# Loads of v issued from POOL, and a later landing counted by a kernel's own scheduler

## The chip, the cores and the metric

The kernel runs on one core of one Trainium2 chip. Its engines are PE (matrix products), DVE (vector), ACT (activations), POOL and SP; each works through its own instructions strictly in order, and instructions on different engines wait for one another by semaphores. SP computes nothing here: its queue issues DMA transfers. The metric is the device time of one execution in microseconds; lower is better.

## The reference

What is computed is chunked local attention over 4 batches of 8 heads with 768 positions, and behind it two feed-forward layers (the names say "moe", but there is one expert):

```python
for c in range(nc):                      # chunks of 32 queries, 16 positions left, 8 right, 8 memory slots
    q_c = q[:, :, c_start:c_end]
    k_full = np.concatenate([mem_k, k[:, :, l_start:r_end]], axis=2)
    v_full = np.concatenate([mem_v, v[:, :, l_start:r_end]], axis=2)
    scores = scale * np.matmul(q_c, k_full.transpose(0, 1, 3, 2))
    a = np.exp(scores - np.max(scores, axis=-1, keepdims=True))
    a = a / (np.sum(a, axis=-1, keepdims=True) + 1e-09)
    out[:, :, c_start:c_end] = np.matmul(a, v_full)
x = out.transpose(0, 2, 1, 3).reshape(3072, 512)
x = (mish(x @ w_in1)) @ w_out1           # 512 -> 2048 -> 512; mish(h) = h * tanh(log(1 + exp(h)))
x = (h * sigmoid(1.702 * h)) @ w_out2    # h = x @ w_in2; 512 -> 2048 -> 512
```

## The kernel before

**Stages.** The 3072 tokens are cut into 8 blocks of 384. In the first phase, attention of the later blocks and the first product of layer 1 run side by side: `forward(j, f)` multiplies block j with column group f of w_in (16 groups), so this phase has 128 units, numbered i = 16 j + f; a unit is two halves of 6 matmuls (from block 1 on), accumulated in a bank `h`, copied to a tile `z` or `gl` (L1262, L1263, on ACT or DVE) and stored to DRAM as `g1d`. Behind it come the second product of layer 1 (L1393), the first of layer 2 (L1292) and the second of layer 2 (L1485), each by a seven-product scheme that needs sums and differences of weights. Products take a float32 operand as two parts, high and low, hence three matmuls for one product.

**Attention, from block 2 on.** `pair_of_heads` loads q and k in pieces (`z_...` and `wo_...` tiles; L364) and turns them on DVE (L658, L662); the few memory keys are copied in by POOL or DVE (L668). PE makes scores (L779), DVE adds the mask and finds the maximum (L837), ACT takes exponentials (L852), DVE or ACT scales them (L872, L880), PE turns the result (L983), and PE multiplies it with v (L1005). `values_of` loads v for half of the heads of a block: a tile `vt`, of which there are two, filled by 8 transfers (four of 120 rows of v, four of 8 memory rows; 10 at the sequence's end), 98 in all.

**Weights.** Beside it, the weights of the other three products are prepared on DVE, two tiles `v` and `u` at a time: shifts and ors (L408 to L422, L422 being the last), a store of both to DRAM (`wd`, SP), and then four sums or differences (L467) that overwrite what was stored, so that the first L467 must wait until the store has been read out of the tile; then a second pair of stores. Nine such groups fall between 97 and 350 us of the trace; two more groups are split on the chip and not stored.

**What sets the order.** Nothing is ordered by hand. The code adds operations to a `Plan` with a rank (in the first phase the number of the unit by which they are wanted), an engine or two to choose from, and a duration. `Plan.issue` walks through a clock of its own, gives each free engine the ready operation of lowest rank, and writes the instructions out in the order of the planned starts. A transfer in it occupies its issuing queue (0.475 us on SP), then a common bus, and whoever waits for it is ready a fixed time behind the bus: 1.1 us. Buffers are given back the same way. On the chip only the orders per engine are left of this plan; the times are the chip's. `CALM = 110` separates the first phase (ranks below it) from the rest.

Of the kernel before, what the change touches and what calls it, by code (L numbers as in the profile page):

```python
# [22 lines left out]
AHEAD = 6  # L23
CUT = 6
URGENT = 4
STAGGER = 1.5
LATE = 3

# [95 lines left out]
class Plan:  # L124
# [12 lines left out]
    def add(self, rank, ways, reads=(), writes=(), updates=(), chain=None, table=None):  # L137
        op = Op()
        op.table = table
        op.rank, op.seq = rank, len(self.ops)  # L140
        lap = self.OVERLAP if rank < self.CALM else {}
        op.ways = [(w[0], max(w[1] - lap.get(w[0], 0.0), 0.06), *w[2:]) for w in ways]
        op.after, op.at = [], 0.0
        need = {}

        def wait(o, lag=True):
            need[id(o)] = (o, lag or need.get(id(o), (o, False))[1])

        for b in (*reads, *updates):
            for o in b.writers:  # L150
                wait(o)
        for b in (*writes, *updates):
            for o in b.readers:
                wait(o)
            b = b.whole
            if not b.users and b.tag is not None:
                if b.inside is not None and b.inside.tag.made[0] is not b.inside:
                    below = b.inside.tag.made
                    k = below.index(b.inside)
                    b.gate += [(o, True) for o in below[k - 1].users]  # L160
                    below[k - 1].closed = True
                made = b.tag.made
                k = made.index(b)
                if isinstance(b.tag, Spread) and k < b.tag.bufs:
                    b.gate += [(o, True) for o in b.tag.before.get(b.inside, ())]
                if k >= b.tag.bufs:
                    b.gate += [(o, True) for o in made[k - b.tag.bufs].users]
                    made[k - b.tag.bufs].closed = True
                if k:
                    b.gate.append((made[k - 1].users[0], False))  # L170
        for b in writes:
            for o, lag in b.whole.gate:
                wait(o, lag)
        for b in updates:
            b.writers, b.readers = [], []
        for b in (*writes, *updates):
            b.writers.append(op)
        for b in reads:
            b.readers.append(op)
        for b in (*reads, *writes, *updates):  # L180
            assert not b.whole.closed
            b.whole.users.append(op)
            if b.whole.inside is not None:
                assert not b.whole.inside.closed
                b.whole.inside.users.append(op)
        if chain is not None:
            if chain:
                wait(chain[-1], False)
            chain.append(op)
        op.need = len(need)  # L190
        for o, lag in need.values():
            o.after.append((op, lag))
        self.ops.append(op)
        return op

    def issue(self):
        engines = ("pe", "act", "dve", "pool", "sp")
        free = dict.fromkeys(engines, 0.0)
        ready = {e: [] for e in engines}
        load = dict.fromkeys(engines, 0.0)  # L200
        coming = []
        bus = 0.0
        for op in self.ops:
            if op.need == 0:
                heapq.heappush(coming, (0.0, op.seq, op))
            op.start = None
        left = len(self.ops)
        now = 0.0
        table = None
        order = []  # L210
        while left:
            while coming and coming[0][0] <= now + 1e-9:
                op = heapq.heappop(coming)[2]
                for w, (e, dur, *_) in enumerate(op.ways):
                    heapq.heappush(ready[e], (op.rank, op.seq, w, op))
                load[op.ways[0][0]] += op.ways[0][1]
            for e in engines:
                if free[e] > now + 1e-9:
                    continue
                kept = []  # L220
                pick = other = None
                while ready[e]:
                    item = heapq.heappop(ready[e])
                    op, w = item[3], item[2]
                    if op.start is not None:
                        continue
                    if w:

                        e0, d0 = op.ways[0][:2]
                        if max(free[e0] - now, 0.0) + load[e0] - d0 < op.ways[w][1] - d0 + 0.3:  # L230
                            kept.append(item)
                            continue
                    if e == "act" and op.table not in (None, table):

                        if other is None:
                            other = item
                        else:
                            kept.append(item)
                        continue
                    pick = item  # L240
                    break
                if other is not None and (pick is None or other[0] + self.PATIENCE < pick[0]):
                    pick, other = other, pick
                if other is not None:
                    kept.append(other)
                for item in kept:
                    heapq.heappush(ready[e], item)
                if pick is None:
                    continue
                op, w = pick[3], pick[2]  # L250
                e_, dur, fn, *size = op.ways[w]
                op.start, op.way = now, w
                load[op.ways[0][0]] -= op.ways[0][1]
                order.append(op)
                left -= 1
                end = now + dur
                if e == "act" and op.table not in (None, table):
                    if table is not None:
                        end += self.RELOAD
                    table = op.table  # L260
                free[e] = end
                lag = self.LAG.get(e, 0.0)
                if op.rank < self.CALM:
                    lag += self.OVERLAP.get(e, 0.0)
                if size:
                    bus = max(bus, end + 0.9) + size[0]
                    end, lag = bus, 1.1
                for o, far in op.after:
                    t = end + lag if far else (now + 0.01 if not size else now + 0.01)
                    o.at = max(o.at, t)  # L270
                    o.need -= 1
                    if o.need == 0:
                        heapq.heappush(coming, (o.at, o.seq, o))
            times = [coming[0][0]] if coming else []
            times += [free[e] for e in engines if free[e] > now + 1e-9]
            if not times:
                assert not left, "operations wait for one another"
                break
            now = min(t for t in times if t > now) if any(t > now for t in times) else now
        order.sort(key=lambda o: (o.start, o.seq))  # L280
        for op in order:
            op.ways[op.way][2]()
# [15 lines left out]
def kernel(  # L298
# [14 lines left out]
    B, H, S, D = q.shape  # L313
# [4 lines left out]
    P = 128  # L318
# [6 lines left out]
    GB = TB // GQ  # L325
# [6 lines left out]
    HV = H // 2  # L332
# [10 lines left out]
    add = plan.add  # L343
# [12 lines left out]
    for f in range(NF):  # L356
        T.update(tags(sb, **{f"{n}{f}": 1 for n in ("wi", "wo")}))

    def load(rank, buf, parts, nbytes, run, reads=(), early=False):

        for part in parts:
            def go(queue, part=part):
                o, i = part()
                queue.dma_start(out=o, in_=i)  # L364

            size = bus(nbytes / len(parts), run)
            ways = [
                ("sp", 0.475, lambda go=go: go(nc.sync), size),
                ("pool", 1.2, lambda go=go: go(nc.gpsimd), size),
            ]  # L370
            add(rank, ways if early else ways[:1], reads=reads, writes=[buf])

# [311 lines left out]
    def values_of(j, hq, rank):  # L686

        b, s0 = divmod(j * TB, S)
        vt = T["vt"].new([P, GB, HV, D], F32)
        parts = []  # L690
        for i in range(GB):
            parts += windows(v, mem_v, b, s0 + i * GQ - LEFT, hq * HV, HV, vt, i)
        load(rank, vt, parts, P * GB * HV * D * 4, 256)
        return vt

    def windows(src, mem, b, t0, h0, nh, tile, i):
# [274 lines left out]
    def oct_out(j, rank, vt, heads):  # L971

        kept = []
        for hp, names, es, late in heads:
            aTs = []
            for n, e in enumerate(es):
# [7 lines left out]

                r = rank + late + STAGGER * n
                add(r + 2.2, [("pe", 0.33, turn)], reads=[e, ident], writes=[t])
# [648 lines left out]
```

## Time and profile before

| | us |
|---|---|
| median of 3 runs | 1133.25 (1132.56 to 1134.08) |
| the profiled execution, its own time | 1132.64 |
| its span, first to last instruction | 1130.3 |
| PE busy | 1101.3 (97%) |
| DVE busy | 855.3 (76%) |
| ACT busy | 593.9 (53%) |
| POOL busy | 14.6 (1%) |

PE is busy nearly throughout; what a change of order can move is the rest of its span. The mean granted TensorE clock is 0.994. The queue that SP fills carries 215.76 MB in 297759 packets, the one that POOL fills 0.75 MB in 352 packets, all of that in the first 15 us, where seven loads of block 0 go through POOL.

### The profile page before, as it was taken

The page shows a single profiled execution, that of the slowest core. Times are in us where ns is not written, and L with a number is a line of the kernel's source. Part 1 is how long each engine was busy: PE and PEld are TensorE (multiplying, and loading weights), DVE is VectorE, ACT ScalarE, POOL GpSimd, SP SyncE. Part 2 cuts the span into 40 slices and gives each one's busy share as a digit, 9 for nine tenths or more (in the row PEclk, how much of TensorE's full clock was granted, in tenths as well). Part 3 has the DMA queues.
Part 4 walks back from the last instruction along what each step waited for, and adds up shares of the span by engine and source line. Part 5 has one row for each costly group of instructions (what it writes and reads, how often), then busy time and mean ns, then how long its engine had stood idle before and what let it go on. Part 6 is the DMA issues. An engine that isn't in the chain of part 4 may idle for free.

```text
span 1130.3 us, 22386 instructions
## 1 busy us (share of the span) xinstructions
PE 1101.3 (97%) x8226; PEld 1060.7 (94%) x8226; DVE 855.3 (76%) x1887; ACT 593.9 (53%) x1375; POOL 14.6 (1%) x29
## 2 busy tenths in 40 slices
PE   7999998999999999999999999999999999999998
PEld 5668898988899999999999999999999999999998
DVE  5997776977676678888897875757557787777875
ACT  5875664764574435555545565555565532333332
POOL 2001000000000000000000000000000000000000
PEclk8999999999999999999999999999999999999999
DMA  9987788878776747546633577777778645436351
GB/s 171 264 235 168 192 213 230 213 193 210 230 234 229 228 143 249 164 140 211 221 114 105 166 255 237 268 254 249 256 229 268 199 114 147 134 107 165 104 155 52
DMA packets 298220, 217.93 MB, mean 193 GB/s; under 512 B 136120, under 2 KB 276423, under 8 KB 298111
## 3 DMA queue, kind: packets, MB, share of 16 engines
q1 hardware_dynamic: 297759, 215.76, 65.0%
q8 instruction: 64, 1.05, 0.4%
q0 software_dynamic: 352, 0.75, 0.4%
q14 instruction: 45, 0.37, 0.1%
HBM read 135.18 MB, written 81.26 MB: 191 GB/s over the span
## 4 chain that ended last, share of the span: by engine, by line
PE 79%; DVE 8%; DMA 6%; SPq 4%; issue 2%; ACT 1%; DVEq 0%; ACTq 0%
PE h L1130 14%; PE o L1485 9%; PE o L1393 9%; PE h L1292 8%; PE o L1292 7%; PE h L1485 6%; PE h L1393 6%; PE s L1485 6%; PE s L1393 6%; SPq L364 4%; PE s L1292 4%; DMA vt<-in_v_dram 2%; DMA wi<-in_moe_w_in_dram 1%; PE o L1005 1%; PE s L779 1%
## 5 line engine op out<-in xcount | busy, mean ns | idle before, releaser
L1130 PE MATMUL h<-xh,wi 128*128 128x384 f32 x640 | 165.7, 340 | 2.7 <-ACT z L1262 1.6
L1130 PEld LDWEIGHTS h<-xh,wi 128*128 128x128 f32 x640 | 114.0, 188 | 4.6 <-ACT z L1262 2.0
L1130 PE MATMUL h<-xl,wi 128*128 128x384 f32 x320 | 107.5, 336 | 0.0
L1130 PE MATMUL h<-wo,wi 128*128 128x384 f32 x384 | 70.9, 339 | 1.2 <-ACT gl L1262 1.2
L1130 PEld LDWEIGHTS h<-wo,wi 128*128 128x128 f32 x384 | 66.1, 188 | 2.1 <-ACT gl L1262 1.5
L852 ACT ACTIVATE e<-e,mx 96x128 f32<-96x128 f32 x144 | 55.9, 392 | 10.8 <-DVE mx L837 10.6
L1130 PEld LDWEIGHTS h<-xl,wi 128*128 128x128 f32 x320 | 60.2, 188 | 0.0
L1262 ACT ACTIVATE z<-h 128x384 f32<-128x384 f32 x47 | 22.9, 487 | 56.9 <-PE h L1130 48.5
L1262 ACT ACTIVATE e<-h 128x384 f32<-128x384 f32 (+2 forms) x47 | 22.4, 477 | 47.3 <-PE h L1485 28.8
L1475 DVE TENSOR_TENSOR xl<-vt,xh 128x1024 fp32r<-128x1024 f32 x24 | 29.3, 1223 | 19.7 <-ACT xh L1472 17.5
L1485 PE MATMUL o<-wo,xh 128*128 128x256 f32 x232 | 43.8, 282 | 0.0
L852 ACT ACTIVATE ev<-ev,mx 96x128 f32<-96x128 f32 x112 | 43.4, 390 | 0.0
L1475 DVE TENSOR_TENSOR xl<-wi,xh 128x1024 fp32r<-128x1024 f32 x32 | 38.8, 1223 | 5.3 <-ACT xh L1472 4.1
L1262 ACT ACTIVATE gl<-h 128x384 f32<-128x384 f32 x45 | 21.9, 486 | 38.6 <-PE h L1130 30.0
L1393 PE MATMUL o<-xh,wo 128*128 128x256 f32 x224 | 40.5, 282 | 0.0
L1376 DVE TENSOR_TENSOR xl<-z,xh 128x1024 fp32r<-128x1024 f32 x24 | 29.2, 1223 | 11.3 <-ACT xh L1372 10.3
L837 DVE CUSTOM_DVE_ANT_0 e<-s,mask 96x128 f32<-96x128 f32 x104 | 24.5, 281 | 16.9 <-PE s L821 11.5
L1472 ACT ACTIVATE xh<-wi 128x1024 fp32r<-128x1024 f32 x25 | 26.4, 1056 | 19.0 <-PE h L1485 8.3
L1485 PEld LDWEIGHTS o<-wo,xh 128*128 128x128 f32 x232 | 36.0, 191 | 0.0
L1393 PEld LDWEIGHTS o<-xh,wo 128*128 128x128 f32 x224 | 34.7, 190 | 0.0
L1485 PE MATMUL o<-wo,xl 128*128 128x256 f32 x116 | 32.8, 283 | 0.0
L1393 PE MATMUL o<-xl,wo 128*128 128x256 f32 x112 | 31.6, 283 | 0.0
(427 smaller groups left out, 3310.7 us busy)
## 6 DMA issues: line engine op xcount, KB each, us to landing
st<-in_moe_w_out_dram SPq DMA_DIRECT2D x32, 512.0 KB
st<-wd SPq DMA_DIRECT2D x29, 512.0 KB
g1d<-z SPq DMA_DIRECT2D x64, 192.0 KB
g1d<-gl SPq DMA_DIRECT2D x64, 192.0 KB
z<-g1d SPq DMA_DIRECT2D x24, 512.0 KB
vt<-gd SPq DMA_DIRECT2D x24, 512.0 KB
wi<-gd SPq DMA_DIRECT2D x24, 512.0 KB
wi<-in_moe_w_in_dram SPq DMA_DIRECT2D x16, 512.0 KB
```

The lines of the kernel that those rows point to most:

```text
L364: queue.dma_start(out=o, in_=i)
L779: nc.tensor.matmul(out=s[hh][:, keys(d, i, True), :], lhsT=queries(d, i), rhs=keys(d, i), start=True, stop=True,)
L837: nc.vector.tensor_tensor_reduce(out=e[:, i, hh, :], in0=s[hh][:, first + i, :], in1=mask[:GQ, mask_of(g0 + i), :], scale=-scale, scalar=-NEG,
L852: nc.scalar.activation(out=e[:, i, hh, :], in_=e[:, i, hh, :], func=AF.Exp, scale=-1.0, bias=mx[:, i, hh:hh + 1], accum_out=sm[:, first + ...
L1130: nc.tensor.matmul(out=h.get(), lhsT=a[:, c], rhs=b.at(kk), start=(n == 0), stop=(n == KD * len(prods) - 1))
L1262: ("act", act(n, True), lambda: nc.scalar.activation(out=dst(), in_=bank.get(), func=AF.Copy)),
L1292: nc.tensor.matmul(out=bank.get(), lhsT=a, rhs=b, start=(fresh and m == 0), stop=(m == 3 * K2 - 1), skip_group_check=not fresh,)
L1376: add(rank + 0.05, [("dve", dve(n2), lambda gh=gh, gl=gl, src=src: nc.vector.tensor_tensor(out=flat(gl), in0=flat(src), in1=flat(gh), op=A ...
L1393: nc.tensor.matmul(out=bank[:, d, :], lhsT=a, rhs=b[:, p, :], start=(fresh and h == d == p == m == 0), stop=(h == 1 and p == HP - 1 and m ...
L1472: ("act", act(NP * P), lambda: nc.scalar.activation(out=flat(gh), in_=flat(src), func=AF.Copy)),
L1475: add(rank + 0.05, [("dve", dve(NP * P), lambda: nc.vector.tensor_tensor(out=flat(gl), in0=flat(src), in1=flat(gh), op=ALU.subtract))], re ...
L1485: nc.tensor.matmul(out=bank.get(), lhsT=a[:, p], rhs=b, start=(fresh and p == 0 and m == 0), stop=(p == NP - 1 and m == 2), skip_group_che ...
```

## The change

There are two edits. `values_of` passes `via="pool"`, and `load` then gives its transfers POOL as their only queue, planned at 0.8 us each. And in `Plan.issue` whoever waits for a transfer of a rank below 110 is counted ready 5 us behind the bus instead of 1.1 (`LANDING`). No operation is added or taken away and no waiting rule changes; since the orders are worked out from the plan, they change on all engines in the first phase.

```diff
+LANDING = 5
...
                 if size:
                     bus = max(bus, end + 0.9) + size[0]
-                    end, lag = bus, 1.1
+                    end, lag = bus, LANDING if op.rank < self.CALM else 1.1
...
-    def load(rank, buf, parts, nbytes, run, reads=(), early=False):
+    def load(rank, buf, parts, nbytes, run, reads=(), early=False, via=None):
...
                 ("sp", 0.475, lambda go=go: go(nc.sync), size),
                 ("pool", 1.2, lambda go=go: go(nc.gpsimd), size),
             ]
-            add(rank, ways if early else ways[:1], reads=reads, writes=[buf])
+            add(rank, [("pool", 0.8, *ways[1][2:])] if via else ways if early else ways[:1], reads=reads, writes=[buf])
...
-        load(rank, vt, parts, P * GB * HV * D * 4, 256)
+        load(rank, vt, parts, P * GB * HV * D * 4, 256, via="pool")
```

Lines of the changed kernel are one higher than before (L364 is L365 there). SP issues 98 transfers fewer and POOL 98 more; PE's order is the same up to the units just before i = 26, differs by single moves of attention work from there, and is the same again behind the first phase, as DVE's, ACT's and SP's are from some way into the second product of layer 1. Three places follow.

SP, ahead of the stores `wd` of the fourth stored group of weights (near 186 us of the trace), before:

```order
L364 DMA vt<-in_v_dram 120x4x64
L364 DMA g1d<-gl 128x384
L364 DMA vt<-in_mem_v_dram 8x4x64
L364 DMA vt<-in_v_dram 120x4x64
L364 DMA vt<-in_mem_v_dram 8x4x64
L364 DMA wo_388<-in_k_dram 32x13x32
L364 DMA g1d<-z_631 128x384
L364 DMA wo_388<-in_k_dram 32x13x32 x2
L364 DMA g1d<-gl 128x384
L364 DMA wd<-v 128x256
```

and the same stores in the changed kernel:

```order
L365 DMA g1d<-z_631 128x384
L365 DMA wo_383<-in_q_dram 32x12x32 x3
L365 DMA g1d<-gl 128x384
L365 DMA wo_383<-in_q_dram 32x12x32
L365 DMA wo_383<-in_k_dram 32x13x32 x4
L365 DMA wd<-v 128x256
L365 DMA wd<-u 128x512
```

The loads of v that stood ahead of the stores are gone from this queue.

DVE, the first stored group of weights (near 110 to 116 us), before:

```order
L414 TENSOR_SCALAR u<-u 128x512
L418 SCALAR_TENSOR_TENSOR v<-st,v 128x512
L418 SCALAR_TENSOR_TENSOR u<-st,u 128x512
L422 SCALAR_TENSOR_TENSOR v<-st,v 128x512
L422 SCALAR_TENSOR_TENSOR u<-st,u 128x512
L467 TENSOR_TENSOR v<-v 128x256
L837 ISA e,mx<-s_1395,mask 96x128
```

and in the changed kernel, where the line of three dots leaves out fifteen of the sixteen mask operations (L838), with their reads of the maximum, and two subtractions:

```order
L423 SCALAR_TENSOR_TENSOR v<-st,v 128x512
L423 SCALAR_TENSOR_TENSOR u<-st,u 128x512
L1025 CAST wo_1436<-o_1389 128x384
L838 ISA e,mx<-s_1398,mask 96x128
...
L1264 COPY gl<-h 128x384
L468 TENSOR_TENSOR v<-v 128x256
L659 STREAM_TRANSPOSE wo_1059<-wo_383 128x384
```

The sum that waits for the store has moved behind a whole round of mask operations.

PE, the third transposition of scores of its round (near 191 us), before:

```order
L1130 MATMUL h<-wo_1711,wi_1102 128x384 x2
L1130 MATMUL h<-wo_1729,wi_1102 128x384
L983 MATMUL o_2487<-ident,ev 128x96 x4
L983 MATMUL o_2495<-ident,ev 128x96 x4
L1130 MATMUL h<-xh,wi_532 128x384 x2
L1130 MATMUL h<-xl,wi_532 128x384
```

and in the changed kernel:

```order
L1131 MATMUL h<-xh,wi_532 128x384 x2
L1131 MATMUL h<-xl,wi_532 128x384
L984 MATMUL o_2506<-ident,ev 128x96 x4
L984 MATMUL o_2515<-ident,ev 128x96 x4
L1131 MATMUL h<-xh,wi_609 128x384 x2
L1131 MATMUL h<-xl,wi_609 128x384
```

The two transpositions have moved behind a whole unit of `forward` (12 matmuls on `wi_532`).

## Rows read from the trace of the kernel before

**Rows 1.** Stretches: length; busy time of PE, PEld, DVE, ACT, POOL; granted clock; DMA share.
```profile
97.00:300.00 203.00, 190.54 (x1526) 179.87 (x1525) 154.94 (x640) 119.87 (x454) 3.43 (x11) 0.99 0.79 206
192.00:197.00 5.00, 5.00 (x56) 4.43 (x56) 1.37 (x3) 0.92 (x2) 0.00 (x0) 0.66 0.91 236
300.00:1130.00 830.00, 824.90 (x6116) 820.48 (x6115) 620.99 (x937) 407.78 (x698) 0.00 (x0) 1.00 0.59 187
```

**Rows 2.** PE in order of time: start, length, instruction [idle before <- releaser].
```profile
121.08 0.62 PE L1130 MATMUL h<-xh,wi 128*128 128x384 f32 x2 [1.07 <-DVE gl L1263]
...
141.63 0.55 PE L983 MATMUL s<-ident,e 96*128 96x96 f32 x4 [1.05 <-DVE e L872]
...
190.75 1.15 PE L983 MATMUL o<-ident,ev 96*128 96x96 f32 x8 [2.99 <-DVE ev L872]
...
236.65 1.15 PE L983 MATMUL o<-ident,ev 96*128 96x96 f32 x8 [1.51 <-DVE ev L872]
...
270.42 0.62 PE L1130 MATMUL h<-xh,wi 128*128 128x384 f32 x2 [1.65 <-ACT z L1262]
...
292.88 3.42 PE L1130 MATMUL h<-wo,wi 128*128 128x384 f32 x18 [1.19 <-ACT gl L1262]
...
297.40 0.55 PE L983 MATMUL s<-ident,e 96*128 96x96 f32 x4 [1.10 <-DVE e L872]
```

**Rows 3.** DVE in order of time, its waits for transfers.
```profile
115.83 0.43 DVE L467 TENSOR_TENSOR v<-v 128x256 f32<-128x256 f32 x1 [4.57 <-DMA wd<-v]
...
139.61 0.42 DVE L467 TENSOR_TENSOR v<-v 128x256 f32<-128x256 f32 x1 [1.01 <-DMA wd<-v]
...
188.26 0.43 DVE L467 TENSOR_TENSOR v<-v 128x256 f32<-128x256 f32 x1 [4.04 <-DMA wd<-v]
...
234.21 0.58 DVE L658 STREAM_TRANSPOSE wo<-z 128x384 f32<-128x384 f32 x1 [3.15 <-DMA z<-in_q_dram]
...
268.83 0.42 DVE L467 TENSOR_TENSOR u<-u 128x256 f32<-128x256 f32 x1 [5.49 <-DMA wd<-u]
...
290.52 0.42 DVE L467 TENSOR_TENSOR u<-u 128x256 f32<-128x256 f32 x1 [4.69 <-DMA wd<-u]
```

**Rows 4.** One group of weights: last preparing instruction on DVE, its store on SP.
```profile
259.44 0.68 DVE L422 SCALAR_TENSOR_TENSOR u<-st,u 128x512 int32<-128x512 int32 x1
...
266.26 0.38 SPq L364 DMA_DIRECT2D wd<-v  x1
```

**Rows 5.** SP's issues of v, 87 to 320 us: count, min/median/max ns, first and last.
```profile
L364 SPq DMA_DIRECT2D vt<-in_v_dram x50: 325/328/1486, 92.7 to 316.8; - x50
L364 SPq DMA_DIRECT2D vt<-in_mem_v_dram x48: 272/377/1375, 93.1 to 317.1; - x48
```

**Rows 6.** DVE groups, 97 to 320 us: count | busy us, mean ns | idle before.
```profile
L837 DVE CUSTOM_DVE_ANT_0 ev<-o,mask 96x128 f32<-96x128 f32 x84 | 19.1, 281 | 0.0
...
L1263 DVE COPY gl<-h 128x384 f32<-128x384 f32 x10 | 5.5, 547 | 4.2 <-PE h L1130 4.2
```

**Rows 7.** The chain that ended last, three pieces: start, us, what.
```profile
256.82 2.11 PE h L1130 x12
258.93 1.47 PE o L1005 x32
...
304.53 1.47 PE o L1005 x32
```

**Rows 8.** POOL's own issues at the start: count, min/median/max ns.
```profile
L364 POOL DMA_DIRECT2D vt<-in_v_dram x2: 587/782/976, 2.7 to 3.3; - x2
...
L364 POOL DMA_DIRECT2D vt<-in_mem_v_dram x1: 580/580/580, 6.0 to 6.0; - x1
```

**Rows 9.** A POOL copy, and what DVE ran meanwhile (in order of time).
```profile
86.56 4.19 POOL L668 COPY wo<-z 128x32 f32<-128x32 f32 x1 [2.63 <-DVE wo L662]
...
88.19 2.48 DVE L523 TENSOR_TENSOR wi<-wo,wi 128x512 fp32r<-128x512 f32 x4
```

**Rows 10.** POOL's copies of memory keys: count, min/median/max ns, first and last.
```profile
L668 POOL COPY wo<-z x8: 209/350/4192, 77.8 to 296.5; 128x32 f32<-128x32 f32 x8
```

## The prediction

> **What bounds the kernel now.** I read the stretches first [rows 1]. PE is busy for 824.90 of the 830 us behind 300 us, so nothing is to be had there; of the 29.0 us that PE idles in all (1130.3 - 1101.3) some 11 lie in the first 97 us, but PE's order is the same there before and after, and SP's differs only from about 75 us on. What the change can reach is the stretch from 97 to 300 us: 203.00 - 190.54 = 12.46 us of idle PE, and a piece at 192 to 197 us in which PE ran at a granted clock of 0.66, part of it therefore at 1.2 instead of 2.4 GHz, after it had stood still for 2.99 us [rows 2]. That piece costs 5.00 x (1 - 0.66) = 1.7 us. The whole stake is 14.2 us.
>
> Next I read PE's own waits there [rows 2]. Seven of them sum to 10.56 us; four smaller ones and single short gaps make up the other 1.90. The releasers are DVE (scaled scores, L872, or the copy of a bank) and ACT (the copy of a bank). These engines are not short of time: DVE is busy for 154.94 of 203 us. So the third view is what DVE waited for [rows 3], and it fits one to one: ahead of every large wait of PE, by 1 to 8 us, DVE stood still for a transfer. Five of the six rows are the first L467 of a group of weights, which must not overwrite a tile before its store has read it; one is a load of q. DVE runs in order, so scaling and copies queued behind that instruction came late, PE after them; ACT's late copies are the same thing one step on, since ACT's queue holds exponentials that wait for DVE's maxima.
>
> Why the store was late is seen in one group [rows 4]: the last preparing instruction ended at 260.12, SP issued the first store at 266.26, 6.1 us later, and the second behind it; DVE went on at 268.83. Some 2 us are the transfer, and the larger part is SP's queue, which is filled with issues end to end. **So the bound is PE, and what it loses here it loses to a wait of DVE for SP's queue.**
>
> **The change part by part.** *v off SP.* SP loses 98 issues: 50 x 0.328 + 48 x 0.377 = 34.5 us at the medians [rows 5], or 4 x 0.328 + 4 x 0.377 = 2.8 us out of each group of 8. What stands behind a group, stores of weights and loads of q and k, is issued that much earlier where the queue is full. On POOL the same transfers cost more, but POOL has 3.43 us of work in the stretch [rows 1]. Its own issues took 0.587 to 0.976 us for v and 0.580 us for memory rows [rows 8]; the longer of the two v loads moves 960 pieces of 256 bytes, those moved now 480, so I take the middle, 0.78: 50 x 0.78 + 48 x 0.58 = 67 us, between 57 and 77. A group of 8 is 4 x 0.78 + 4 x 0.58 = 5.4 us. Who waits for it? v is wanted late: there are two `vt` tiles, so a load starts when the product two groups back ends (258.93 + 1.47) and is read two products later, at 304.53 [rows 7]: 44 us, of which 5.4 and a landing are used. Behind the group on POOL's queue stand the copies of memory keys and a clearing of a tile; a group waits at the head of the queue for its `vt`, and who is behind it waits too; but the scores that need those copies come a product later, 22.8 us ((304.53 - 258.93) / 2), against 5.4 for a group. I cost this part at nothing on the path; what it costs if that cover is gone is the third rival.
>
> *A later landing in the plan.* No transfer gets slower; what waits for one is written further down. The order shows it where DVE waited: in the first stored group, no instruction stood between the preparation and the first L467, and now a round of 16 mask operations, a cast, two subtractions and a copy do. With 19.1 / 84 = 0.227 us for a mask operation and 0.547 for each of the others [rows 6] that is 16 x 0.227 + 4 x 0.547 = 5.8 us of work against a wait of 4.57. In the groups at 268.83 and 290.52 the mask operations ahead go from 4 and 2 to 16 and one copy is added: 12 x 0.227 + 0.55 = 3.3 and 14 x 0.227 + 0.55 = 3.7 us more, against 5.49 and 4.69; with 2.8 us from SP's queue both are covered, or short by a few tenths. At 188.26 the work put ahead of the sum and the work taken away nearly cancel, and I count neither; but PE's transposition has itself moved behind one unit of `forward`, 2.11 us [rows 7], so 4.04 meets 2.8 + 2.1. At 139.61 the wait is 1.01 and SP's 2.8 us alone outweigh it. At 234.21 neither DVE's nor PE's order changes in my favour; there only SP's relief works.
>
> *Sum.* Recovered: 1.07 (121.08), 1.05 (141.63), 2.99 (190.75) and the 1.7 of the low clock behind it, half of 1.51 (236.65), 1.65 (270.42), 1.19 and 1.10 (292.88, 297.40), and 1.0 of the 1.90 in small gaps: 12.5 us. Moving work later can open a wait that was not there: I take off one of mean size, 10.56 / 7 = 1.5. That leaves 11.0. The profiled execution took 1132.64, 0.6 below the median of the runs; I subtract from the median: 1133.25 - 11.0 = **1122.3 us**. The ends of this case are the full stake, 1133.25 - 14.2 = 1119.0, less 0.7 for the spread of the runs, 1118.3; and three such new waits, 1126.
>
> **The rule that speaks against it.** One POOL copy took 4.19 us while DVE ran two-input operations back to back, and it ended with the last of them, at 90.75 against 90.67 [rows 9]; the shortest of its eight took 0.209 [rows 10]. The Trainium skill, page SBUF — State Buffer, section SBUF: two separate sides, says that a transfer issued from POOL can be starved in this way, because DVE in certain modes keeps POOL from writing the descriptors, and advises issuing from SP or ACT. By that rule v lands late; what it would take for that to reach PE is the third rival.
>
> **The rivals.** *Half of it.* Stalls move rather than vanish: PE's rounds now start later, and DVE meets the same transfers nearer to PE's need. For it: the order before, too, was worked out so that PE should wait for nothing here, and the chip did not follow. Half of 12.5 gives 1133.25 - 6.2 = 1127.0. Chance 0.2.
>
> *Waits change their name.* The recovered waits come back in full as waits for exponentials or maxima of rounds that start one unit later: 1133, within 0.2% of before (about what a measurement of this kernel can tell from no change). Against it: DVE has 48 us of idle time in the stretch. Chance 0.1.
>
> *Slower: POOL falls behind.* The place is POOL's queue. Products of v come every 22.8 us, and POOL must issue 8 transfers in that time, so it decides at a mean of 2.85 us an issue. The stretched copy [rows 9] says that such lengths occur beside DVE; the issues of [rows 8] ran while DVE was hardly busy. At 3.3 us each group loses 26.4 - 22.8 = 3.6 us, ten groups 36, less the 44 - 26 = 18 us of slack of the first: PE waits some 18 us, and with the 11 recovered the time is 1140. Against it: the median of the same eight copies is 0.350 us [rows 10], beside a DVE that is busy three quarters of the time. Chance 0.12, some of it for a loss by the new order alone.
>
> **How the numbers follow.** Forecast (1118.3 to 1126) 0.58; half 0.20; no change 0.10; slower 0.12. Faster by over 0.2%: 0.58 + 0.20 = 0.78. The range runs from 1118.3 over the second case to 1131.5, which leaves out the last two cases but a little.
>
> **What would show it.** Right: in 97 to 300 us PE's idle time falls from 12.46 to about 3, no piece at a granted clock near 0.66, the waits of L468 for `wd` are under 2 us each, POOL's v issues lie between 0.58 and 0.98 us. Wrong: new waits of PE for L984's or L1131's inputs of over 1 us, products L1006 that wait for `vt`, POOL issues of over 2 us, or DVE operations longer than before in the same rows.

## The result, and the profile after

The changed kernel took **1118.86 us** (median of 4 runs, 1114.36 to 1119.53) against 1132.9 for the kernel before beside it: a ratio of 0.9869, 95% interval 0.984 to 0.9899. A second series gave 1119.94 us (5 runs) and 0.9878 (0.9857 to 0.9899). On the scale of 1133.25 us that is a gain of 13.8 to 14.8 us. The forecast was 1122.3, a gain of 11.0: the sign was right, the gain a quarter to a third larger than forecast, at the very end of the range (1118.3).

The head of the page of the kernel after, busy time by engine:

```profile
span 1117.3 us, 22424 instructions
...
PE 1095.4 (98%) x8226; PEld 1057.9 (95%) x8226; DVE 861.3 (77%) x1894; ACT 590.8 (53%) x1368; POOL 77.5 (7%) x127
```

The span fell by 13.0 us (from 1130.3), PE's busy time by 5.9 (from 1101.3). So not only idle time went. Stretches of the kernel after, with the columns of [rows 1]; the second runs from the start of the first matmul of unit i = 18 to that of unit i = 88:

```profile
97.00:300.00 203.00, 200.26 (x1656) 192.52 (x1655) 174.09 (x707) 124.14 (x464) 61.90 (x100) 1.00 0.85 224
...
100.17:300.76 200.59, 197.85 (x1641) 190.11 (x1641) 172.02 (x690) 121.73 (x451) 58.88 (x95) 1.00 0.85 224
```

And the same work, i = 18 to i = 88, in the kernel before:

```profile
99.33:314.21 214.88, 202.42 (x1642) 191.21 (x1641) 163.50 (x673) 127.37 (x464) 3.43 (x11) 0.99 0.80 210
```

A stretch bounded by the same work on both sides can be subtracted: 214.88 - 200.59 = 14.3 us, so the whole gain arises here. (Unit 18 starts 0.84 us later than before, what follows unit 88 keeps a lead of some 12.4 to 13.5 us, and the end comes 13.0 us earlier.) Of the 14.3, idle PE accounts for 12.46 - 2.74 = 9.7 and PE's *busy* time for 202.42 - 197.85 = 4.6, at equal counts. PE's waits after, in order of time, as in [rows 2]:

```profile
161.75 0.52 PE L984 MATMUL o<-ident,e 96*128 96x96 f32 x4 [0.37 <-ACT e L881]
...
224.59 0.61 PE L1131 MATMUL h<-xh,wi 128*128 128x384 f32 x2 [0.73 <-ACT gl L1263]
...
262.06 0.62 PE L1131 MATMUL h<-xh,wi 128*128 128x384 f32 x2 [0.77 <-DVE gl L1264]
...
264.13 0.52 PE L984 MATMUL s<-ident,e 96*128 96x96 f32 x4 [0.73 <-ACT e L881]
```

None of the seven waits of [rows 2] is left, and four small new ones stand there. Who waited for the stores `wd`, 97 to 300 us, before (us in all, times):

```profile
  DVE u L467: 17.1, 6
  DVE v L467: 11.7, 4
```

and after:

```profile
  DVE v L468: 2.8, 2
  DVE u L468: 2.2, 1
```

So DVE's waits for stores, the large ones of [rows 3] and smaller ones, fell from 28.8 to 5.0 us. The largest that is left, one store on SP and the sum that waits for it, beside [rows 4]:

```profile
256.72 0.38 SPq L365 DMA_DIRECT2D wd<-u  x1
...
260.32 0.43 DVE L468 TENSOR_TENSOR u<-u 128x256 f32<-128x256 f32 x1 [2.18 <-DMA wd<-u]
```

POOL's issues of v after, 87 to 320 us, to be set beside SP's in [rows 5] and POOL's own in [rows 8]:

```profile
L365 POOL DMA_DIRECT2D vt<-in_v_dram x50: 571/789/809, 91.2 to 302.1; - x50
L365 POOL DMA_DIRECT2D vt<-in_mem_v_dram x48: 555/555/601, 92.0 to 302.7; - x48
```

None is long, though DVE is busy for 172.02 of 200.59 us around them, with two-input operations such as L524 (the L523 of [rows 9]) among what it ran. No wait of PE names `vt`. From issue to landing these transfers took 2.4 to 7.9 us; for SP the trace of before gives no such figure, so a later landing isn't ruled out.

The rule of the Trainium skill weighed in the prediction (page SBUF — State Buffer, section SBUF: two separate sides) ties the starving to operations of DVE in a two-port mode, and this kernel hardly puts it to the test. DVE's quickest operations for their size, L409 and L415 (0.42 us for 128x512, against 0.69 for L419), never ran while one of the 98 issues did. In the kernel with landing 8 (below) they met: an issue of POOL, the L409 inside it, and an L415 beside two other issues.

```profile
255.98 1.00 POOL L365 DMA_DIRECT2D vt<-in_mem_v_dram  x1
...
256.45 0.42 DVE L409 TENSOR_SCALAR u<-st 128x512 f32<-128x512 f32 x1
...
279.09 0.70 DVE L415 TENSOR_SCALAR u<-u 128x512 int32<-128x512 int32 x1
```

Two issues of memory rows took 1.00 and 0.96 us there instead of 0.555, both with an L409 inside, and the L415 took 0.70 instead of 0.42. That agrees with the rule, though that these operations run in such a mode is not shown, and with landing 3 one issue (at 271.72) kept its 0.555 with an L409 inside. A meeting cost at most some 0.45 us; that the changed kernel has none is an accident of its order.

**Where the 4.6 us of busy time come from.** 1.7 are the low clock of [rows 1], gone with the wait of 2.99 us ahead of it. The rest are waits inside PE's busy time. Before, ACT scaled four pieces and PE turned them (two views of the kernel before, by engine):

```profile
251.00 1.28 ACT L880 ACTIVATE e<-e,r 96x128 f32<-96x128 f32 x4 [0.80 <-DVE r L798]
...
251.68 0.97 PE L983 MATMUL s<-ident,e 96*128 96x96 f32 x4
```

and the same step after:

```profile
240.43 1.27 ACT L881 ACTIVATE e<-e,r 96x128 f32<-96x128 f32 x4
...
242.58 0.49 PE L984 MATMUL s<-ident,e 96*128 96x96 f32 x4
```

Four transpositions take 0.49 us when their pieces are ready, and 0.97 when PE arrives while ACT is still scaling and takes them at ACT's pace. No row of PE shows idle time there: each piece's modelled span fills the time until the next. Over the stretch the 160 transpositions, each counted from where nothing ahead of it runs any more (added up from the single records of the two traces), took 17.23 us before and 14.08 after: 3.1 us, against the 2.9 that are left of 4.6 once the clock's 1.7 are taken off.

### The profile page after: what moved, and what is told of

Read it like the earlier page. It is cut to its first block, busy times and chain, and to the rows that moved or that the text cites. A ratio compares the mean times of both kernels' runs of the same rounds, so it can differ in the third digit from the quotient of the medians.

```text
span 1117.3 us, 22424 instructions
## 1 busy us (share of the span) xinstructions
PE 1095.4 (98%) x8226; PEld 1057.9 (95%) x8226; DVE 861.3 (77%) x1894; ACT 590.8 (53%) x1368; POOL 77.5 (7%) x127
## 4 chain that ended last, share of the span: by engine, by line
PE 88%; DMA 4%; DVE 4%; SPq 2%; ACT 1%; issue 1%; DVEq 0%; ACTq 0%
PE h L1131 20%; PE o L1486 9%; PE o L1394 9%; PE h L1293 9%; PE o L1293 7%; PE h L1486 6%; PE h L1394 6%; PE s L1486 6%; PE s L1394 6%; PE s L1293 4%; SPq L365 2%; PE o L1006 1%; PE o L1131 1%; DMA wi<-in_moe_w_in_dram 1%; PE s L780 1%; PE o L780 1%
## 5 line engine op out<-in xcount | busy, mean ns | idle before, releaser
L365 POOL DMA_DIRECT2D vt<-in_v_dram x52 | 40.7, 782 | 97.9 <-PE o L1006 78.5
L1476 DVE TENSOR_TENSOR xl<-vt,xh 128x1024 fp32r<-128x1024 f32 x24 | 29.4, 1224 | 21.2 <-ACT xh L1473 19.0
L1263 ACT ACTIVATE gl<-h 128x384 f32<-128x384 f32 x40 | 19.6, 490 | 47.7 <-PE h L1131 37.7
L1476 DVE TENSOR_TENSOR xl<-wi,xh 128x1024 fp32r<-128x1024 f32 x32 | 38.8, 1223 | 5.3 <-ACT xh L1473 4.5
L838 DVE CUSTOM_DVE_ANT_0 e<-s,mask 96x128 f32<-96x128 f32 x104 | 24.2, 281 | 17.9 <-PE s L822 10.9
L1473 ACT ACTIVATE xh<-wi 128x1024 fp32r<-128x1024 f32 x25 | 26.4, 1057 | 19.6 <-PE h L1486 9.1
```

Source lines behind the costliest of these rows:

```text
L838: nc.vector.tensor_tensor_reduce(out=e[:, i, hh, :], in0=s[hh][:, first + i, :], in1=mask[:GQ, mask_of(g0 + i), :], scale=-scale, scalar=-NEG,
L1263: ("act", act(n, True), lambda: nc.scalar.activation(out=dst(), in_=bank.get(), func=AF.Copy)),
L1473: ("act", act(NP * P), lambda: nc.scalar.activation(out=flat(gh), in_=flat(src), func=AF.Copy)),
L1476: add(rank + 0.05, [("dve", dve(NP * P), lambda: nc.vector.tensor_tensor(out=flat(gl), in0=flat(src), in1=flat(gh), op=ALU.subtract))], re ...
```

## The experiments

Columns: median and ratio to the kernel before beside it; then, from one profiled run, the length of the stretch from i = 18 to i = 88 and PE's busy time in it.

| kernel | us | ratio (95%) | i = 18 to 88 | PE busy |
|---|---|---|---|---|
| before | 1131 to 1133 | 1 | 214.88 | 202.42 |
| after | 1118.86 | 0.9869 (0.984 to 0.9899) | 200.59 | 197.85 |
| after, second series | 1119.94 | 0.9878 (0.9857 to 0.9899) | 203.08 | 199.10 |
| v on POOL, landing 1.1 | 1124.44 | 0.9936 (0.9915 to 0.9956) | 207.47 | 200.12 |
| v on SP, landing 5 | 1128.93 | 0.9978 (0.9966 to 0.9991) | 204.06 | 198.74 |
| order of after, v on SP | 1130.18 | 0.9992 (0.9977 to 1.0008) | 211.81 | 204.20 |
| order of before, v on POOL | 1121.25 | 0.9923 (0.9901 to 0.9944) | 204.63 | 199.79 |
| landing 5 for `wd` alone | 1123.28 | 0.9915 (0.9896 to 0.9934) | 204.12 | 197.53 |
| landing 5 for all but `wd` | 1127.03 | 0.9935 (0.9915 to 0.9956) | 205.94 | 200.70 |
| landing 3 | 1117.31 | 0.9858 (0.9837 to 0.9879) | 200.46 | 197.79 |
| landing 8 | 1132.68 | 0.9993 (0.9981 to 1.0005) | 209.38 | 200.60 |
| landing 5, all phases | 1202.08 | 1.0627 (1.0596 to 1.0658) | 198.44 | 196.95 |
| landing 5, ranks to 128 | 1122.76 | 0.9918 (0.9902 to 0.9934) | 200.65 | 197.14 |
| landing 3, ranks to 128 | 1116.72 | 0.9868 (0.9853 to 0.9883) | 201.86 | 199.09 |
| 4 clearings on POOL | 1127.58 | 0.9967 (0.9955 to 0.998) | 210.06 | 200.51 |
| 6 clearings | 1147.61 | 1.0136 (1.0113 to 1.0159) | 227.34 | 205.53 |
| 8 clearings | 1169.13 | 1.0323 (1.0302 to 1.0344) | 248.78 | 208.25 |
| 16 clearings | 1367.74 | 1.2079 (1.2057 to 1.2101) | | |

The last two columns come from one execution of each kernel, and it can lie some us from the median beside it: 1133.56 with 4 clearings, 1143.23 with 6, 1126.95 with landing 5 for `wd` alone.

### Each edit alone, and the order apart from the queue

Each diff is against the changed kernel. v on POOL alone:

```diff
-LANDING = 5
+LANDING = 1.1
```

> The loads of v go to POOL, and the plan counts 1.1 us for every landing, as before: the first edit alone, with the order that the plan makes of it. My theory (PE loses what DVE loses to the stores of weights, which stand in SP's full queue; both edits shorten that wait): SP's relief of 2.8 us a group recovers about half, idle PE in 97 to 300 us near 6 us, time 1125 to 1128. Rival, the order does it all: 1131 to 1134, waits of the sums for the stores as long as before. Rival, the queue does it all: 1118 to 1120.

The later landing alone:

```diff
-        load(rank, vt, parts, P * GB * HV * D * 4, 256, via="pool")
+        load(rank, vt, parts, P * GB * HV * D * 4, 256)
```

> The plan counts 5 us for a landing in the first phase, and v is loaded from SP as before: the second edit alone. My theory: about half, 1123 to 1127, sums behind a round of mask operations, but stores still late in SP's queue. Rival, the order does it all: 1118 to 1120. Rival, the queue does it all: 1131 to 1134.

All engines' orders of the changed kernel, but v is issued by SP:

```diff
-            add(rank, [("pool", 0.8, *ways[1][2:])] if via else ...
+            add(rank, [("pool", 0.8, lambda go=go: go(nc.sync), size)] if via else ...
```

> Every engine's order is that of the changed kernel, worked out with v on POOL, but the transfers of v are issued by SP, at the place where the plan starts them. It tells the queue apart from the order, with the order held. My theory: some 2.8 us more of waiting where 8 issues stand ahead of a store; the order covers most of it, 1119 to 1123. Rival, the queue is the main thing: 1125 or more. Rival, the order does it all: as the changed kernel, 1118 to 1119.5.

The orders of the kernel before, but v is issued by POOL:

```diff
-LANDING = 5
+LANDING = 1.1
...
-            add(rank, [("pool", 0.8, *ways[1][2:])] if via else ...
+            add(rank, [("sp", 0.475, *ways[1][2:])] if via else ...
```

> The order of every engine is that of the kernel before, worked out with v on SP, but the transfers of v are issued by POOL at their places. My theory: stores leave SP up to 2.8 us earlier, the sums stand right behind the preparation as before, half of the waits go: 1125 to 1129. Rival, the queue is the main thing: 1118 to 1121. Rival, the order does it all: 1131 to 1134.

What DVE waited for, 97 to 315 us (us in all, times, longest). The order of after, v on SP:

```profile
DVE v L468 <- DMA wd<-v: 8.3, 4, 3.6
DVE u L468 <- DMA wd<-u: 4.3, 3, 2.9
```

The order of before, v on POOL:

```profile
DVE u L468 <- DMA wd<-u: 13.1, 5, 5.0
DVE v L468 <- DMA wd<-v: 4.3, 2, 3.4
```

v on POOL with a plan of its own:

```profile
DVE u L468 <- DMA wd<-u: 11.5, 4, 7.2
DVE v L468 <- DMA wd<-v: 2.7, 1, 2.7
```

The later landing alone, v on SP:

```profile
DVE wo L659 <- DMA z<-in_q_dram: 5.7, 1, 5.7
DVE gl L1264 <- DMA g1d<-gl: 2.7, 1, 2.7
...
DVE u L468 <- DMA wd<-u: 1.3, 1, 1.3
```

The queue and the order form a table of two by two: 1 with neither, 0.9923 with POOL under the old order, 0.9992 with the new order on SP, 0.987 with both. By ratio, POOL is worth 8.7 us under the old order and 13.4 under the new one; the new order is worth nothing that can be measured on SP and 5 to 6 us on POOL. My expectations, about half the gain for each part, were too high for the later landing alone (1128.9 against 1123 to 1127) and for the new order on SP (1130.2 against 1119 to 1123), and too low for POOL under the old order (1121.3 against 1125 to 1129) and, by little, for POOL with a plan of its own (1124.4 against 1125 to 1128). The time doesn't follow the sum of DVE's waits for `wd`: it is 12.6 us with the order of after on SP (1130.2) and 17.4 with the order of before on POOL (1121.3). What counts is which of them reach PE, which idles for 7.6 and 4.8 us in the stretch of the table. So among these four kernels SP's full queue is the main cause, and the order made for POOL gives its share only with v off SP: it puts the reader of a store later, but the store itself waits in SP's queue.

That is not true of every later order. The later landing alone has an order that the plan made for v on SP, and it takes nearly all waits away from `wd` (1.6 us are left) and lets some turn up at the loads of q, which stand on the same queue. Between i = 18 and i = 88 it is 10.8 us shorter than the kernel before, more than v on POOL with landing 1.1 (7.4). Its profile leads the kernel before by 9.2 us at i = 88 (314.21 - 304.99) and by 4.7 at the end (1130.3 - 1125.6). What is lost lies at one place behind the stretch, SP's issue of a load, ACT's wait for it and PE's wait for ACT:

```profile
310.26 0.39 SPq L365 DMA_DIRECT2D z<-g1d  x1
...
314.65 1.06 ACT L1356 ACTIVATE z<-z 128x1024 f32<-128x1024 f32 x1 [3.96 <-DMA z<-g1d]
...
316.14 2.29 PE L1131 MATMUL h<-wo,wi 128*128 128x384 f32 x6 [3.29 <-ACT gl L1263]
```

The load stands behind transfers of v on SP's queue, and the granted clock from 316 to 322 us is 0.72. So the small gain of this kernel hangs on one wait, in one profile; that a later order is worth little without POOL is not shown in general.

The new order on SP also shows what a wait costs beyond itself. PE's wait in that kernel, and the stretch behind it:

```profile
166.51 0.88 PE L984 MATMUL o<-ident,e 96*128 96x96 f32 x4 [2.87 <-ACT e L881]
```

```profile
166.00:171.00 5.00, 4.49 (x18) 4.52 (x19) 4.99 (x18) 3.12 (x14) 0.58 (x2) 0.50 0.92 252
```

A granted clock of 0.50 is 1.2 GHz throughout. PE is busy for 4.49 us of this stretch, at half its speed, so by my estimate the stretch alone loses 2.2 us, not much less than the 2.87 of the wait ahead of it.

### The changed kernel again, and which landings count

> The changed kernel once more, beside the runs it is compared with below. Its four runs stood at 0.987 of before; with before at 1131 to 1133 both theories expect 1116 to 1119.

It came out at 1119.94, a little above the expectation. Its profile is 2.5 us longer between i = 18 and i = 88 than the first one, and all of that arises at one place: the wait of 0.37 us at 161.75 is 1.68 here, and the clock falls behind it. PE's wait, and the stretch, second profile of the kernel after:

```profile
162.69 0.52 PE L984 MATMUL o<-ident,e 96*128 96x96 f32 x4 [1.68 <-ACT e L881]
```

```profile
164.00:166.00 2.00, 2.00 (x8) 2.00 (x7) 2.00 (x9) 1.19 (x6) 0.21 (x1) 0.50 1.02 342
```

So a difference of 2 us between single profiles of two kernels means nothing here; the ratios of the medians decide.

Only the stores of weights counted late (v on POOL):

```diff
+        op.late = False                      # for a new operation
...
-                    end, lag = bus, LANDING if op.rank < self.CALM else 1.1
+                    end, lag = bus, LANDING if op.late and op.rank < self.CALM else 1.1
...
+            plan.ops[-1].late = True         # behind each store wd
```

> v issued by POOL, and of the transfers only the stores of prepared weights (wd) counted as landing after 5 us; all others after 1.1. With v on POOL alone the profile kept 11.5 us of DVE waits for wd<-u, and one PE gap of 3.3 us behind the longest of them. Theory A: the later landing earns its share at these stores alone, since L468 waited for them; then this kernel is as fast as the changed one, within 2 us (1117 to 1120). Theory B: the gain of the later landing comes from other transfers (loads of q, k and the turned tiles z and g1d), whose readers no longer stand at the head of a queue; then it is no faster than v on POOL alone, 1123 to 1126.

All but these stores (the same edit with `True` and `False` exchanged):

> The complement: v issued by POOL, and every transfer but the stores wd counted as landing after 5 us. Theory A: the waits of L468 for wd<-u stay, as with v on POOL alone, and the time is 1123 to 1126. Theory B: 1117 to 1120. If both this and its complement are near 1121, the share is spread over all transfers.

Neither theory holds. Counted for the stores alone the later landing is worth 2.4 us over v on POOL alone (0.9915 against 0.9936; the intervals overlap, so this is not clear of noise), for all others nothing (0.9935), for both some 7 us (0.9874, the middle of the two series). The orders that come out differ as wholes; the share can't be put down to one kind of transfer.

Then the value. 8 instead of 5:

```diff
-LANDING = 5
+LANDING = 8
```

> The changed kernel with 8 us in place of 5 as the landing that the plan counts. In the changed kernel PE is idle for 2.74 us in 97 to 300 us, so there is at most that to gain. Theory 'covered': what waits is already written far enough down, the time stays within 0.2% of the changed kernel, 1117 to 1121. Rival 'too late': work that others need is pushed behind what it fed, PE waits for L872 or L1263 again and the time goes up by one to three gaps of 1.5 us, 1121 to 1124.

3 instead of 5:

```diff
-LANDING = 5
+LANDING = 3
```

> The changed kernel with 3 us in place of 5 as the landing that the plan counts. So far, with v on POOL: 1.1 gave a ratio of 0.9936, 5 gave 0.987 to 0.988, 8 gave 0.9993. Theory 'there is a best value near what the chip takes': a gain between the first two, 0.988 to 0.993, 1119 to 1125. Rival 'the plan's result jumps with any value, and 5 is a lucky draw': anything from 0.987 to 1.0, above all a value worse than that of 1.1.

1.1, 3, 5 and 8 give 0.9936, 0.9858, 0.987 to 0.988 and 0.9993. With 3 the gain is that of 5, more than the 1119 to 1125 that I expected; with 8 it is gone, by more than either expectation said. Two rows of the kernel with 8, one from who waited for `wd` on DVE, one of PE's waits in order of time:

```profile
  DVE u L468: 0.9, 1
```

```profile
351.89 0.62 PE L1131 MATMUL h<-xh,wi 128*128 128x384 f32 x2 [2.83 <-ACT gl L1263]
```

DVE hardly waits for stores any more, and PE waits instead, mostly for the copies of its banks. This is the prediction's second rival, waits that change their name, at a larger dose. How long the chip takes can be read at a store whose reader does stand waiting. v on POOL with 1.1, in order of time:

```profile
257.97 0.44 SPq L365 DMA_DIRECT2D wd<-u  x1
...
263.32 0.42 DVE L468 TENSOR_TENSOR u<-u 128x256 f32<-128x256 f32 x1 [7.18 <-DMA wd<-u]
```

From the start of SP's issue to the reader it is 5.3 us here and 3.6 in the kernel after (256.72 to 260.32). In the kernel before, the sum at 268.83 in [rows 3] waits for the second store of its group:

```profile
266.73 0.40 SPq L364 DMA_DIRECT2D wd<-u  x1
```

That is 2.1 us. All three are stores of 128 KB. The plan's own figure for such a store, with the bus free, is 0.475 for the issue, 0.9 ahead of the bus, 0.45 on it (131072 bytes at 290 a ns) and the landing: 2.9 us with 1.1, 4.8 with 3, 6.8 with 5, 9.8 with 8. So 1.1 covers one of the three places, 3 covers two and 5 all of them; 3 gained as much as 5 all the same, and 8 writes the reader later than any of the three needed. Three places argue for a landing of 3 to 5 us; they don't prove it.

### Counted in more of the kernel

In all phases:

```diff
-                    end, lag = bus, LANDING if op.rank < self.CALM else 1.1
+                    end, lag = bus, LANDING
```

> The changed kernel with the landing of 5 us counted in all phases, not in the first alone. Behind 410 us the changed kernel's PE waits only a few times, 2 to 3 us in all, so there is hardly anything to gain there. Expected: within 0.3% of the changed kernel, 1116 to 1122. Rival: the plan writes work too late there, as it did in the first phase with 8 us, and PE waits: 1122 to 1130.

For all ranks of the first phase, with 5 and with 3 us:

```diff
-                    end, lag = bus, LANDING if op.rank < self.CALM else 1.1
+                    end, lag = bus, LANDING if op.rank < 128 else 1.1
```

> The changed kernel with the landing of 5 us counted for all ranks of the first phase (below 128, not 110), and 1.1 behind it. Theory 'last units': with the landing in all phases the forward unit i = 88 began 3.2 us earlier than in the changed kernel; this kernel has that too and ends at 1114 to 1117. Theory 'later work': that came from work of the next phase written into the first, and this kernel is as the changed one, 1117 to 1121.

> The same with 3 us instead of 5. With ranks below 110 the value 3 gave 1117.3, not to be told from 5. Theory 'last units': 1113 to 1117; theory 'later work': 1116 to 1120.

In all phases the kernel loses 6%: I had expected no difference, and its rival at most 1130. The first phase is as good as ever (198.44 us from i = 18 to 88); all is lost behind 410 us, most of it behind 890. Stretches of this kernel, and one group of PE's waits there:

```profile
640.00:890.00 250.00, 232.93 (x1259) 222.35 (x1259) 137.69 (x275) 126.53 (x268) 0.00 (x0) 0.98 0.65 215
890.00:1190.00 300.00, 266.71 (x2038) 262.84 (x2037) 196.34 (x214) 92.39 (x139) 0.00 (x0) 0.93 0.41 117
```

```profile
PE o L1486 <- DVE xl L1476: 10.2, 5, 2.3
```

In the last phase PE waits once a step for the tiles that L1473 and L1476 make on ACT and DVE from what the step's load brings, and the clock falls after it. Nothing was short there with 1.1; why these tiles come later than PE needs them was not followed further.

The two kernels with ranks to 128 show no gain in the first phase over the changed one (200.65 and 201.86 us), so the theory of the last units falls. The 3.2 us by which i = 88 came earlier with all phases are little more than the 2.5 us between two profiles of one kernel, and stay open. With 5 us and ranks to 128 the whole (1122.76, above both expectations) is 0.4 to 0.5% slower than the changed kernel, and its profile loses that behind 410 us. With 3 it is not to be told from the changed kernel; nor is 3 with ranks below 110. No kernel here beats the changed one by more than the intervals.

### POOL made late

The third rival: n clearings of a tile that nobody reads, 128x128, behind each transfer of v on POOL. The plan knows nothing of them, so all orders stay.

```diff
+    filler = sb.tile([P, P], F32, name="filler")
...
                 queue.dma_start(out=o, in_=i)
+                if via:
+                    for _ in range(n):
+                        nc.gpsimd.memset(filler, 0.0)
```

> The changed kernel, with 8 clearings of an unused 128x128 tile on POOL behind each transfer of v (work added that the plan does not know of). At 0.205 us a clearing the mean per issue goes from 0.68 to 2.3 us, below the 2.85 us from which the prediction's third rival decides: no more than 0.3% above the changed kernel, 1117 to 1123. Rival: a clearing takes longer beside a busy DVE, as one copy of POOL did, or the slack is smaller than worked out; then PE waits for vt already here, 1125 or more.

> The same with 16 clearings: 0.68 + 16 x 0.205 = 4.0 us an issue, above 2.85. By the prediction's formula a group of 8 loses 31.7 - 22.8 = 8.9 us, ten groups 89, less 18 of slack: 71 us, some 1190, with POOL busy throughout the stretch and the products L1006 waiting for vt. If the cover is larger than worked out, clearly less than 71 us; with a threshold anywhere above 4.0 us an issue, as the changed kernel.

> The changed kernel with 4 clearings on POOL behind each transfer of v. From start to start a clearing took 0.26 us, so an issue takes 0.68 + 4 x 0.26 = 1.7 us and a group of 8 some 14 us, against 20 to 23 us from product to product. Theory 'a point': no loss, within 0.3% of the changed kernel, 1116 to 1123. Theory 'any delay counts' (a straight line from 0 at none to the 50 us of 8 clearings): 1144.

> The same with 6 clearings: 2.24 us an issue, 18 us a group, still below the 20 us between the first products. Theory 'a point': 1117 to 1128, with a wait or two where products stand closest. Theory 'any delay counts': 1157.

With 4, 6, 8 and 16 clearings the time is 1127.58, 1147.61, 1169.13 and 1367.74 us. A clearing took 0.26 us from start to start, so an issue takes some 1.7 us with 4 of them, 2.2 with 6 and 2.8 with 8. The loss begins below 1.7, far ahead of the prediction's point of 2.85 us, without a jump, though not on a straight line through the 8 clearings either (8, 28 and 50 us over 1119.4; 11, 30 and 51 by the ratios). So neither 'a point' (1116 to 1123 with 4, 1117 to 1128 with 6) nor 'any delay counts' (1144 and 1157) came true, and with 16 the loss is 248 us where the prediction's formula gave 71.

For the wait that the prediction meant, PE for `vt`, the point is not far off: with 4 and 6 clearings no wait of PE names `vt`. With 8, at 2.8 us an issue, and with 16 these do (97 to 420 us, a fence each):

```profile
PE o L1011 <- DMA vt<-in_mem_v_dram: 3.2, 2, 1.9
PE s L1011 <- DMA vt<-in_mem_v_dram: 2.8, 1, 2.8
```

```profile
PE o L1011 <- DMA vt<-in_mem_v_dram: 33.7, 4, 9.1
PE s L1011 <- DMA vt<-in_mem_v_dram: 27.6, 4, 9.1
```

But another wait comes before it and costs more. What SP waited for from 97 us on, with 4, 6 and 8 clearings (one fence each):

```profile
SPq L621 <- POOL wo L674: 17.4, 2, 14.2
```

```profile
SPq L621 <- POOL wo L674: 35.2, 2, 26.3
```

```profile
SPq L621 <- POOL wo L674: 53.6, 2, 34.8
```

The 26.3 us in full, with 6 clearings, POOL's and SP's rows:

```profile
108.21 0.79 POOL L367 DMA_DIRECT2D vt<-in_v_dram  x1 [0.52 <-issue]
...
144.44 0.20 POOL L614 MEMSET wo<- 128x128 f32 x1
...
118.25 0.32 SPq L367 DMA_DIRECT2D wd<-v  x1
144.66 0.30 SPq L621 DMA_DIRECT2D wo<-in_mem_k_dram  x1
```

POOL clears the tile of the memory keys (L614; L609 in the kernel after, at 119.39) behind two groups of v, which hold it from 108.21 to 144.44. SP's next instruction is the load into this tile. It waits, and every store and load behind it waits too; DVE, ACT and PE follow (PE idles for 13.88 us, to 147.56).

## Where the prediction held, and which step of it failed

- **The bound and its cause: right in kind.** PE lost in 97 to 300 us by waits of DVE for SP's queue. With v on POOL under the old order 8.7 us come back, though 17.4 us of DVE's waits for stores are left there, so not each of them reached PE, and "one to one" holds for the large ones of the first profile only.
- **The stake: the step that failed.** I took idle PE (12.46) and the low clock (1.7), 14.2 us, as all there was to win, since I read busy PE as work. Some 2.9 us more were waits inside busy time: PE turning pieces at the pace at which ACT made them. The real stake was 12.46 + 1.7 + 2.9 = 17.1. The prediction put waits inside busy time at nothing and gave no reason for it; the transpositions alone show 3.1 us of them (17.23 to 14.08).
- **What comes back: mis-sized.** I counted 10.8 of the idle time (half of the wait of [rows 2] at 236.65, 1.0 of 1.90 in small gaps). None of the old waits is left, so all 12.46 came back. For the load of q at 234.21 in [rows 3] I had said that only SP's relief works. It doesn't do it alone: with v on POOL under the old order most of that wait still stands, and it is gone only with both edits.

```profile
225.78 0.58 DVE L659 STREAM_TRANSPOSE wo<-z 128x384 f32<-128x384 f32 x1 [2.51 <-DMA z<-in_q_dram]
```

- **New waits: mis-sized the other way.** I took off 1.5; the first profile has 2.74 us of idle PE, 2.60 of it in four waits. 12.46 + 1.7 + 2.9 - 2.7 comes to the 14.3 us measured in the same stretch; it must, since the 2.9 are what was left over, and the independent check on them is the 3.1 above. The forecast was 12.5 - 1.5 = 11.0: too small by 2.9 and by 1.7 (12.46 for 10.8), too large by 1.2, so in part the errors cancel.
- **SP's relief against the new order: weighed wrongly.** I let the order cover most of the waits and SP's 2.8 us a group fill in. With that order alone (v on SP) DVE still waits 12.6 us for `wd`, and the time hardly moves. The order that the plan makes for SP leaves 1.6 us of these waits, but loses elsewhere what it gains.
- **POOL's issues: right.** 50 x 0.789 + 48 x 0.555 = 66 us, 67 forecast, and free at this length. The rows weighed against them [rows 9] show a copy beside two-input operations of DVE, which is another case than the two-port modes that the rule speaks of.
- **The cover of POOL: wrong, without harm here.** I let what stands behind a group of v wait 22.8 us, until the scores need it. But the clearing behind it releases a load on SP, and SP holds up everybody. The cover is far shorter, and a loss on POOL's queue was nearer than the third rival put it, though by another path: waits of PE for `vt` do begin near its 2.85 us.
- **The signs named in advance.** Idle PE 2.74 (about 3 forecast); POOL's issues 0.56 to 0.81 us (0.58 to 0.98 forecast); waits for `wd` 1.11, 1.69 and 2.18 (under 2 forecast). No piece of low clock in the first profile; in the second, one behind a wait of 1.68.
- **The rivals.** "Half of it" and "waits change their name" did not happen at 5 us; the latter did at 8.

## What to carry to other kernels

Measure a stake between two instructions that both kernels have, and look for waits inside busy time as well: rows of the same operation that take twice as long in one place as in another. In a kernel ordered by a plan, relieve the queue that is full first; an order made for a relieved queue paid nothing on the full one here, and a safety margin that helps in one phase can cost far more in another. Look also behind the stretch that you measure: one wait there took half of a gain. Before calling a small engine free, follow every instruction behind the new work to who waits for it, up to in-order queues of other engines: the cover of POOL's work here was set by one clearing for which SP waited.

## What was not expected of the hardware

- A short wait of PE was followed by several us at half the clock (1.2 GHz): 2.87 us of wait and then a clock of 0.50 for 5 us, 1.68 and then 0.50 for 2. A wait of 2.17 us in the kernel with landing 5 for `wd` alone, at the same place in the program, was followed by no fall.
- 98 issues of POOL beside a DVE busy for 86% of the stretch took 0.555 to 0.809 us; none was stretched like the copy of [rows 9]. With landing 8 two of them met an L409 of DVE and took 1.00 and 0.96 instead of 0.555.
- A store of 128 KB took 2.1 to 5.3 us from SP's issue until its reader went on, in the three places read.
